# Loading the first FFN weights when the generation ends, and placing inverse units and x loads among the first f-tiles

## The chip, the cores and the metric

One NeuronCore of a Trainium2 chip runs the whole program. The metric is the time of one execution on the device in microseconds (us); the median of three runs is given. Engines are called PE (TensorE), ACT (ScalarE), DVE (VectorE), POOL (GpSimd) and SP (SyncE, which here only issues DMAs).

## The reference

Input `A_u` is 2048 tokens by 640 channels. Two residual blocks follow each other, each behind a layer norm with shift and scale computed from a condition vector `c`:

```python
h = _layernorm(x) * (1 + ca) + sa
x = x + ga * _A_ref(h, ...)      # S4D: causal convolution of h with a generated kernel K
h = _layernorm(x) * (1 + cb) + sb
x = x + gb * _B_ref(h, w1, w3, w2)   # SwiGLU
# A: K = 2 Re sum_n C[d,n] exp(A dt pos), y = irfft(rfft(h) * rfft(K)) + h * D_skip
# B: out = (silu(h @ w1) * (h @ w3)) @ w2      w1, w3: 640 x 1728, w2: 1728 x 640
```

All of it is float32.

## The kernel before

**Convolution.** The channels are taken in five pieces of 128. For each piece the convolution kernel is *generated* on POOL, ACT, DVE and PE (`gen_steps`, matmuls `kps`, L511). `k_steps` then takes its first transform (matmuls `pk`, L574; ACT copies them to `ko`, L578) and stores it to device memory (`k<-ko`, L581, eight DMAs per piece). `freq_steps` (18 steps per piece) loads the transformed input (`ht`) and the kernel (`kt`) back, transforms them further (`fa` L612, `fk` L626), multiplies (`fp`, L628), transforms back (`fa` L616), copies on ACT to `hz` (L618, three buffers) and stores `zd<-hz` (L621). The generation of one piece overlaps with the frequency steps of the piece before it. After the last generation only the last piece's `k` store, its `kt` load and its 18 frequency steps remain.

**Inverse.** The last transform goes by token blocks. A *unit* is two of sixteen groups of tokens: `inverse_load` fetches `iz<-zd` by four DMAs, `inverse` does 16 matmuls `iy` (L655) and adds them to `x2` on DVE (L660), which was loaded by `load_x2` (`x<-in_x`, four DMAs of 320 KB per block). Units 0 and 1, the token block 0, are done in part during the last piece's frequency steps (L927) and finished from `izb` after them. Units 2 and 3 (block 1) stand before the FFN; units 4 to 7 go among its f-tiles.

**FFN.** Four token blocks of 512. `ln2` normalises a block and turns it (`tp`, L692) into a high and a low half (`xh`, `xl`). For each block 14 f-tiles of 128 hidden features, in the order 0, 13, 1, 2, ..., 12 (13 is half a tile): `weights` loads `wr` (w1, w3) and `w2r`, and splits them on ACT (L670) and DVE (L671) into halves; `up` does 15 matmuls for each of w1 and w3 (L758 to L760, tiles `gu` in three PSUM banks); `gate` applies SwiGLU; `down` adds to five accumulators (`acc`, L793 to L799). Raw and split weights have two buffers each. `mid(b, i)` is called after every f-tile and puts inverse units and the next block's `ln2` in between. The weights of the first `WA = 2` f-tiles are loaded ahead.

**What sets the order.** Every instruction carries a priority, set by `self.at(v)`, and a scheduler with a model of the machine's times fixes each engine's order at build time; an engine then works strictly in that order. Lower numbers come first, and `last` is the last piece, number 4. Before the change the weights ahead stand at `1000 * last + 2500`, behind the frequency steps of the last piece (`+ 1000`). `order(a, b)` additionally keeps `a` behind `b` without a wait. All DMAs are issued by SP in one queue, and each issue waits until the one eight places before it has landed, since the DMAs share eight semaphores.

The inverse units' placement hangs on one constant, `IU`: units 2 to `IU - 1` stand before the FFN, the others are called from `mid`, where unit `m + 1` comes behind the f-tile at place `m`:

```python
for u in range(2, IU):
    self.inverse_unit(u, ip, po, None, 1, self.behind)
...
    if b == 0 and IU <= m + 1 < 8:
        self.inverse_unit(m + 1, ip, ps, "gu", 3)
```

Before the FFN the units use the banks of the accumulators (`po`); in `mid` they use the three `gu` banks.

Of the kernel before, what the change touches and what calls it, by code (L numbers as in the profile page):

```python
# [29 lines left out]
AE = '0101'  # L30
EG,EP,EH=[float(v) for v in '-730,-650,-750'.split(",")]
WA = int('2')
IU = int('4')
HU = [int(c) for c in '01234567']
MR = float('-850')
XB = int('4')
# [62 lines left out]
class K:  # L99
# [715 lines left out]
    def run(self):  # L815
# [9 lines left out]
        def open_(name, side=None, bufs=1, space=None):  # L825
            scopes[name] = ExitStack()
            return self.pool(name, bufs=bufs, space=space, ctx=scopes[name], side=side)
# [24 lines left out]
        last = self.param_turn(pp, psg, 0)  # L852
# [33 lines left out]
        last = NB - 1  # L886
# [21 lines left out]
        xp, ip, wp = open_("xp"), open_("ip"), open_("wp")  # L908
        self.x2 += [xp.tile([P, 4, D], F32, name=f"x2{b}") for b in range(1, 4)]
        self.ahead, self.turn = {}, 0  # L910
        mid_load = self.load
        self.at(1000 * last - 40)
        for st in self.k_steps(last, stp, kop, psg, KB, ip):
            st()
# [7 lines left out]
        for u in range(2):  # L922
# [7 lines left out]
            nc.vector.tensor_add(x2, py, x2)  # L930
            for j in (2 * u, 2 * u + 1):
                self.ln_part(stats[0], self.x2[0], j, 0, KT - 1)
        self.at(1000 * last + 2500)
        wload = self.load
        for m in range(WA):
            self.ahead[0, m] = self.weights(0, self.ORDER[m], wp, wload)
        self.at(1000 * last + 3000)
        close("fpool", "wbp", "kop", "ksp")
        pool = open_("ffn", "right")
# [1 line left out]
        po = open_("po", space=PSUM)  # L941
        ps = open_("ps", space=PSUM)
        z = self.inverse_load("izb", ip, "izb", 1, 0, 4, cut, D)
        for b in range(1, 4):
            self.load_x2(b, self.zload)
        self.inverse(0, 4, z, ps, "gu", 3, cut, D)
        nxt = {0: self.ln2(0, pool, ps, stats)}
        self.at(1000 * last + 4000)
        for u in range(2, IU):
            self.inverse_unit(u, ip, po, None, 1, self.behind)  # L950
        self.at(1000 * last + 5000)

        def mid(b, m):
            if b == 0 and IU <= m + 1 < 8:
                self.inverse_unit(m + 1, ip, ps, "gu", 3)
            if m == 8 and b < 3:
                nxt[b + 1] = self.ln2(b + 1, pool, ps)

        self.ffn(nxt, wp, pool, ps, po, mid)
        close("ps", "po", "ffn", "wp", "ip", "xp", "first")  # L960

# [29 lines left out]
```

## Time and profile before

| | |
|---|---|
| median of 3 runs | 1206.31 us (1205.34 to 1208.49) |
| the profiled execution | 1206.96 us, its span 1205.2 us |
| PE busy | 1029.8 us (85%) |
| DVE busy | 696.6 us (58%) |
| ACT busy | 495.2 us (41%) |
| POOL busy | 316.6 us (26%) |
| mean granted PE clock | 0.914 |

The generation ends at about 485 us, the last frequency steps end at 557 us, and the FFN's matmuls run from 582 us to the end. In a profile line, `out<-in` are tile names with buffer numbers left out, `[0.39 <-ACT hz L618]` is idle time before the instruction and what ended it, and SPq is SP's queue of DMA issues.

### The profile page before, as it was taken

How to read it: one execution, taken by the hardware profiler on the slowest of the kernel's cores; microseconds unless marked ns; L12 is line 12 of the kernel's file. 1: busy time of each engine (PE TensorE's matmuls, PEld its weight loads, DVE VectorE, ACT ScalarE, POOL GpSimd, SP SyncE). 2: the span in 40 equal slices, each digit the busy share in tenths (PEclk: the TensorE clock that was granted, in tenths of full speed). 3: DMA queues.
4: the chain of work that ended last, by engine and by line, in shares of the span. 5: the costliest groups of instructions: out<-in, count | busy, mean ns of one | idle time of the engine just before them, and what ended most of it. 6: DMA issues, size and time to landing. Idle time of an engine off the chain costs nothing.

```text
span 1205.2 us, 17828 instructions
## 1 busy us (share of the span) xinstructions
PE 1029.8 (85%) x6737; PEld 777.4 (65%) x6737; DVE 696.6 (58%) x1224; ACT 495.2 (41%) x768; POOL 316.6 (26%) x329
## 2 busy tenths in 40 slices
PE   2357673895996989895699999999999999999996
PEld 0134342673775857674376788888888888888885
DVE  7999979746866763143474484544745445354332
ACT  3456566436456573312242243432424333343221
POOL 5677768645757871000000000000000000000000
PEclk9578785797897988998699999999999999999999
DMA  9957648335365454778956333533335332353311
GB/s 265 232 160 222 184 125 220 86 104 116 95 172 112 114 117 122 175 187 218 214 142 155 97 88 88 136 96 86 97 88 133 108 95 74 84 143 98 98 44 44
DMA packets 206525, 157.61 MB, mean 131 GB/s; under 512 B 56680, under 2 KB 188648, under 8 KB 204776
## 3 DMA queue, kind: packets, MB, share of 16 engines
q1 hardware_dynamic: 206440, 156.48, 49.8%
q8 instruction: 53, 0.87, 0.3%
q14 instruction: 32, 0.26, 0.1%
HBM read 119.74 MB, written 36.70 MB: 130 GB/s over the span
## 4 chain that ended last, share of the span: by engine, by line
PE 70%; DVE 14%; DMA 7%; ACT 3%; issue 2%; SPq 2%; POOL 1%; DVEq 0%; ACTq 0%
PE gu L760 11%; PE gu L758 10%; PE gu L759 10%; PE fk L626 6%; PE fa L616 5%; PE acc L793 5%; PE acc L795 5%; PE acc L794 5%; PE fa L612 3%; PE kps L511 3%; PE iy L655 2%; DMA k<-ko 1%; DMA xt<-in_x 1%; DVE xs L258 1%; DVE step L446 1%
## 5 line engine op out<-in xcount | busy, mean ns | idle before, releaser
L758 PE MATMUL gu<-xh,wh 128*128 128x512 f32 x540 | 214.2, 397 | 0.5 <-ACT xh L695 0.5
L760 PE MATMUL gu<-xh,wl 128*128 128x512 f32 x540 | 213.9, 396 | 0.0
L759 PE MATMUL gu<-xl,wh 128*128 128x512 f32 x540 | 213.9, 396 | 0.0
L670 ACT ACTIVATE wh<-wr 128x640 fp32r<-128x640 f32 x108 | 74.2, 732 | 146.7 <-PE gu L759 134.5
L511 PE MATMUL kps<-yy,xx 128*32 128x64 f32 x2560 | 83.5, 247 | 53.3 <-DVE xx L503 28.3
L511 PEld LDWEIGHTS kps<-yy,xx 128*32 128x32 f32 x2560 | 61.6, 123 | 101.4 <-issue 53.9
L727 POOL MEMSET w2l<- 64x640 f32 x4 | 2.5, 626 | 469.0 <-PE acc L794 469.0
L758 PEld LDWEIGHTS gu<-xh,wh 128*128 128x128 f32 x540 | 101.7, 188 | 26.1 <-issue 1.0
L760 PEld LDWEIGHTS gu<-xh,wl 128*128 128x128 f32 x540 | 101.5, 188 | 26.4 <-issue 2.0
L759 PEld LDWEIGHTS gu<-xl,wh 128*128 128x128 f32 x540 | 101.6, 188 | 24.9 <-issue 0.5
L628 DVE TENSOR_TENSOR fp<-fk,hz 128x512 f32<-128x512 f32 x80 | 54.8, 686 | 98.1 <-PE fk L626 97.8
L626 PE MATMUL fk<-kt,wb 128*128 128x128 f32 x640 | 99.8, 305 | 13.1 <-DMA kt<-k 12.3
L626 PEld LDWEIGHTS fk<-kt,wb 128*128 128x128 f32 x640 | 90.6, 212 | 23.8 <-DMA kt<-k 7.6
L793 PE MATMUL acc<-ah,w2h 128*128 128x512 f32 x260 | 104.6, 402 | 0.0
L794 PE MATMUL acc<-ah,w2l 128*128 128x512 f32 x260 | 102.7, 395 | 0.0
L618 ACT ACTIVATE hz<-fa 128x512 f32<-128x512 f32 (+1 forms) x90 | 49.2, 547 | 126.5 <-PE fa L616 105.6
L487 POOL TENSOR_TENSOR yy<-e,e 128x512 f32<-128x512 f32 x80 | 87.0, 1109 | 42.7 <-PE kps L511 42.7
L795 PE MATMUL acc<-al,w2h 128*128 128x512 f32 x260 | 98.1, 395 | 0.0
L671 DVE TENSOR_TENSOR wl<-wr,wh 128x640 fp32r<-128x640 f32 x108 | 84.5, 817 | 16.6 <-ACT wh L670 16.6
L773 DVE SCALAR_TENSOR_TENSOR a<-th,gu 128x512 f32<-128x512 f32 x52 | 35.7, 687 | 100.3 <-ACT th L772 100.2
L774 DVE TENSOR_TENSOR a<-a,gu 128x512 f32<-128x512 f32 x52 | 35.7, 686 | 94.5 <-PE gu L760 94.5
L772 ACT ACTIVATE th<-gu 128x512 f32<-128x512 f32 x52 | 31.1, 598 | 139.5 <-PE gu L760 139.5
(190 smaller groups left out, 1801.2 us busy)
## 6 DMA issues: line engine op xcount, KB each, us to landing
wr<-in_w SPq DMA_DIRECT2D x104, 320.0 KB, 3.9
w2r<-in_w SPq DMA_DIRECT2D x52, 320.0 KB, 3.0
h<-ho SPq DMA_DIRECT2D x32, 320.0 KB, 4.5
k<-ko SPq DMA_DIRECT2D x40, 256.0 KB, 4.3
ht<-h SPq DMA_DIRECT2D x40, 256.0 KB, 2.8
kt<-k SPq DMA_DIRECT2D x40, 256.0 KB, 3.2
zd<-hz SPq DMA_DIRECT2D x80, 128.0 KB, 1.9
wm<-in_w_mod SPq DMA_DIRECT2D x10, 960.0 KB, 8.4
```

The lines of the kernel that those rows point to most:

```text
L487: G.tensor_tensor(out.rearrange("p d (k i) -> p d k i", k=4), bc(t1, 2, 4), bc(t2, 3, 8), op=ALU.mult)
L511: nc.tensor.matmul(kps[q * 32:(q + 1) * 32, e * 64:(e + 1) * 64], xx[:, r, i, :], yy[:, r, i, :, :].rearrange("p a b -> p (a b)"), start=( ...
L616: nc.tensor.matmul(pa[:, 1], self.wz[:, r, :], pp[:, r], start=(r == 0), stop=(r == 1))
L626: nc.tensor.matmul(pk[:, r, g], self.wb[:, 2 * i + g, r, :], kt[:, g0 + g, :], start=True, stop=True)
L670: self.nc.scalar.activation(H, v, AF.Copy)
L671: eng.tensor_tensor(Lo, v, H.bitcast(F32), op=ALU.subtract)
L758: nc.tensor.matmul(pg, wh[:, i, k, :], xh[:, k, :], start=(k == 0), stop=False)
L759: nc.tensor.matmul(pg, wh[:, i, k, :], xl[:, k, :], start=False, stop=False)
L760: nc.tensor.matmul(pg, wl[:, i, k, :], xh[:, k, :], start=False, stop=(k == KT - 1))
L793: nc.tensor.matmul(acc[k], w2h[:, sl], ah, start=(m == 0), stop=False)
L794: nc.tensor.matmul(acc[k], w2l[:, sl], ah, start=False, stop=False)
L795: nc.tensor.matmul(acc[k], w2h[:, sl], al, start=False, stop=(m == 12))
```

## The change

The weights of the first two f-tiles get the priority `1000 * last - 60`, just before `k_steps` of the last piece, and lose the order behind the last `kt` load. `IU` becomes 2, so that no inverse unit stands before the FFN, and units 2 and 3 are called from `mid` behind the f-tiles at places 1 and 2. The loads of x for blocks 1, 2 and 3 no longer stand between `izb` and the inverse of block 0, but before the FFN (block 1) and in `mid` at places 1 and 3 (blocks 2 and 3). In the program that results, SP issues the x loads of blocks 1 and 2, then the `iz` loads of units 2 and 3, then x of block 3.

```diff
-IU = int('4')
+IU = int('2')
...
         mid_load = self.load
+        self.at(1000 * last - 60)
+        for m in range(WA):
+            self.ahead[0, m] = self.weights(0, self.ORDER[m], wp)
         self.at(1000 * last - 40)
         for st in self.k_steps(last, stp, kop, psg, KB, ip):
             st()
...
-        self.at(1000 * last + 2500)
-        wload = self.load
-        for m in range(WA):
-            self.ahead[0, m] = self.weights(0, self.ORDER[m], wp, wload)
         self.at(1000 * last + 3000)
...
         z = self.inverse_load("izb", ip, "izb", 1, 0, 4, cut, D)
-        for b in range(1, 4):
-            self.load_x2(b, self.zload)
         self.inverse(0, 4, z, ps, "gu", 3, cut, D)
...
+        self.load_x2(1, self.zload)
+
         def mid(b, m):
+            if b == 0 and m in (1, 3):
+                self.load_x2((m + 3) // 2, self.zload)
             if b == 0 and IU <= m + 1 < 8:
                 self.inverse_unit(m + 1, ip, ps, "gu", 3)
```

## The prediction

> **What bounds the kernel now.** I read the chain that ended last first. TensorE (PE) carries most of it, so the question is where PE waits and whether the change reaches those places.
>
> ```profile
> PE 70%; DVE 14%; DMA 7%; ACT 3%; issue 2%; SPq 2%; POOL 1%; DVEq 0%; ACTq 0%
> ```
>
> The list of PE's waits, taken from 480 to 615 us, gives the places (who waited, for what, us in total, times, longest):
>
> ```profile
> PE iy L655 <- DMA izb<-zd: 10.1, 1, 10.1
> PE fk L626 <- DMA kt<-k: 5.6, 1, 5.6
> PE iy L655 <- DMA iz<-zd: 5.4, 1, 5.4
> PE tp L692 <- ACT xn L686: 5.3, 1, 5.3
> ```
>
> After 590 us PE is busy to the end, so each us by which that stretch starts earlier, or finishes with more done, is a us of the time. The chain from 425 to 700 us (start, duration, what) shows what stands in front of it:
>
> ```profile
> 507.00 4.23 DMA kt<-k
> ...
> 554.21 1.85 SPq L705
> ...
> 556.16 5.25 DMA zd<-hz
> ...
> 561.93 1.81 DMA zd<-hz
> ...
> 568.90 9.51 DMA x<-in_x
> 578.42 11.76 DMA iz<-zd
> 590.31 4.50 PE iy L655 x8
> ...
> 597.59 2.30 PE iy L655 x10
> ...
> 601.01 0.68 PE iy L655 x2
> ...
> 604.92 1.76 PE iy L655 x12
> ...
> 646.58 2.31 PE iy L655 x16
> ```
>
> The reader is to see three things: SyncE's queue (SPq) issuing a weight load (L705) directly ahead of the last zd stores; x loads of 9.5 us and iz loads of 11.8 us one behind the other; and 32 inverse matmuls (iy, L655) that PE takes at once, the first eight of them slowly.
>
> **Gain 1: the tail of the last frequency stage.** Before, the first two f-tiles' weights are loaded and split among its last steps. PE's timeline there:
>
> ```profile
> 541.59 1.05 PE L626 MATMUL fk<-kt,wb 128*128 128x128 f32 x8
> ...
> 543.78 1.05 PE L626 MATMUL fk<-kt,wb 128*128 128x128 f32 x8
> ...
> 554.33 1.05 PE L626 MATMUL fk<-kt,wb 128*128 128x128 f32 x8
> 555.22 2.15 PE L616 MATMUL fa<-fp,wz 128*128 128x256 f32 x8
> ```
>
> A step takes 543.78 − 541.59 = 2.19 us when nothing disturbs it. The four steps from 543.78 to 554.33 take 10.55 instead of 8.76 us. With the splits on ScalarE (ACT) and VectorE (DVE) gone from between them, **1.8 us** go.
>
> PE then ends this stage at 557.4, but ACT's last copy comes later, and SP issues the izb loads after it:
>
> ```profile
> 561.52 0.38 ACT L618 ACTIVATE hz<-fa 128x256 f32<-128x256 f32 x1 [2.88 <-DMA zd<-hz]
> ```
> ```profile
> 563.75 2.60 SPq L644 DMA_DIRECT2D izb<-zd  x4
> ```
>
> The copy waits for a buffer that a zd store still reads, and that store stood behind the weight load of 554.21. Without it the copy follows PE: 561.52 − 557.4 = 4.1 us, less some latency, I take **4.0 us**. Everything from izb to the first FFN matmul (DVE and ACT's layer norm, the transposes) moves forward unchanged; the 10.1 us wait shrinks by these 4.0.
>
> **Gain 2: units 2 and 3 leave the start of the FFN.** In the changed program PE goes through all 45 matmuls of f-tiles 0 and 13 before the first inverse matmul, and SP issues eight x loads instead of twelve ahead of that unit's iz loads. The 5.4 us wait for iz goes: its own four loads are done after twelve of 320 KB instead of sixteen, while PE comes to it some 12 us after its FFN start, not one. So **5.4 us**. The 32 inverse matmuls took 4.50 + 2.30 + 0.68 + 1.76 = 9.24 us; a unit of 16 among warm FFN matmuls takes 2.31, so two take 4.62: **4.6 us**.
>
> Against this stands the clock. FFN matmuls start slowly and become fast only after the iy rows:
>
> ```profile
> 582.38 0.79 PE L758 MATMUL gu<-xh,wh 128*128 128x512 f32 x1 [0.49 <-ACT xh L695]
> 582.97 0.63 PE L759 MATMUL gu<-xl,wh 128*128 128x512 f32 x1
> 583.40 0.63 PE L760 MATMUL gu<-xh,wl 128*128 128x512 f32 x1
> ...
> 595.33 0.39 PE L758 MATMUL gu<-xh,wh 128*128 128x512 f32 x1
> 595.56 0.39 PE L759 MATMUL gu<-xl,wh 128*128 128x512 f32 x1
> ```
>
> Spacing is 0.43 us slow and 0.23 fast; from 590.31 PE needed 5.0 us of unbroken work to reach the fast one. By 606.7 (604.92 + 1.76), counting the two programs' order of instructions, 32 FFN and 32 inverse matmuls were done: 606.7 − 582.4 = 24.3 us, of which 24.3 − 5.4 − 9.2 = 9.7 for the FFN ones. After: 5.0 us slow hold 11.6 of them, the other 20.4 take 4.8, so 9.8 us: a loss of **0.1 us**. If the slow stretch ran to 8.5 us the loss would be 1.7. [...]
>
> **Loss 1: where the loads now land.** They are moved to the end of generation, in SP's queue ahead of zd of step 10; the loads of f-tiles 1 and 2 follow as buffers come free, among the k stores. Their sizes, from the issues between 540 and 557 us:
>
> ```profile
> wr<-in_w SPq DMA_DIRECT2D x6, 320.0 KB, 6.5
> w2r<-in_w SPq DMA_DIRECT2D x3, 320.0 KB
> ...
> wr<-in_w SPq DMA_DIRECT2D x2, 160.0 KB
> w2r<-in_w SPq DMA_DIRECT2D x2, 160.0 KB, 6.4
> ```
>
> That is 11 × 320 KB = 3.60 MB. All of it is now queued before the last k store, and all k stores must land before kt can be loaded, for which PE already waits 5.6 us. So every us that the k stores lose is a us on PE. What the DMA engines had free there, by stretches (PE, PEld, DVE, ACT, POOL busy, clock, DMA share, GB/s):
>
> ```profile
> 484.50:493.00 8.50, 8.50 (x42) 6.28 (x43) 1.48 (x3) 4.32 (x6) 0.00 (x0) 1.00 0.44 106
> 493.00:505.00 12.00, 12.00 (x61) 9.11 (x60) 2.77 (x4) 4.25 (x7) 0.00 (x0) 1.00 0.94 197
> 541.00:556.00 15.00, 14.22 (x86) 12.12 (x84) 7.88 (x12) 6.71 (x11) 0.00 (x0) 1.00 0.93 252
> ```
>
> PE's last matmuls of the generation, which let the weights' memory go, are these:
>
> ```profile
> 484.06 0.44 PE L511 MATMUL kps<-yy,xx 128*32 128x64 f32 x12
> ```
>
> So the loads can be issued from 484.5. From 493 on the engines are full; before, 8.5 × 0.56 = 4.8 us are free. At 252 GB/s, the rate where these same loads run today, 3.60 MB take 14.3 us; less 4.8, the k stores and kt come **9.5 us** later. I take this value because its row is that of the same transfers. At 197 GB/s, the rate beside k stores, it is 18.3 − 4.8 = 13.5. Below, the loads could hide wholly (0) if the engines had more room than their share shows. Five splits each are put into ACT's and DVE's queues ahead of ko and fp; at 0.7 us (1.37 for two in ACT's row below) they delay ko by some 3.4 us. In SP's queue the zd stores, ht loads and k stores stand behind loads that wait for a free buffer. Both delays lie inside the wait for the k stores, so I add nothing for them; if the DMA engines were idle meanwhile, they would count (the third rival).
>
> [...]
>
> **Loss 2: PSUM in the FFN.** Unit 2 now takes the three gu banks right behind f-tiles 0 and 13. Its second half needs the bank of f-tile 13, which DVE's L782 frees. Rows of ACT and of DVE:
>
> ```profile
> 609.72 1.37 ACT L670 ACTIVATE wh<-wr 128x640 fp32r<-128x640 f32 x2 [2.60 <-PE gu L759]
> ```
> ```profile
> 607.90 0.48 DVE L660 TENSOR_TENSOR x<-iy,x 128x320 f32<-128x320 f32 x1
> ...
> 613.29 0.69 DVE L782 TENSOR_TENSOR a<-u,gu 64x512 f32<-64x512 f32 x1
> ```
>
> ACT's first row starts when f-tile 13's matmuls end, so its bank is free 613.98 − 609.7 = 4.3 us later, after the change with two adds (L660) more on DVE in front, 5.3. PE has 4 inverse matmuls (0.6) and 15 of the down projection (3.5) in between: a wait of 5.3 − 4.1 = **1.2 us**. From 0, if DVE takes the adds later, to 3, if unit 3 meets it as well. The x loads of blocks 2 and 3 and the iz loads of units 4 on are needed 20 us or more after they are issued: nothing. POOL's clearing of a piece of w2l moves with the weights and POOL is idle there: nothing.
>
> **Sum.** 1.8 + 4.0 + 5.4 + 4.6 = 15.8 gained; 0.1 + 9.5 + 1.2 = 10.8 lost; net −5.0 us. The profiled execution took 1206.96 us (span 1205.2), 0.65 above the median of 1206.31, so 1201.96 in its terms and **1201.3** as a median.
>
> **Rivals.** *Early loads are free*: they go into the idle engines and kt loses 3 us at most, by the share of 0.44. For it: in the chain kt's issue at 507 hangs on SP's queue as well as on the last store. Against: full engines from 493. Time: 1206.3 − 15.8 + 0.1 + 3 + 0 = 1193.6. [...]
>
> *It evens out*: loads run at 197 GB/s (13.5) and the FFN's start waits 3: 0.8 us slower, 1207.1. For it: those k stores, at that rate, are the neighbours.
>
> *Slower: SP's queue*. A load waits in the queue for a buffer that a split must free, and k stores stand behind it while DMA engines idle. SP's row of such a wait today:
>
> ```profile
> 544.65 2.66 SPq L705 DMA_DIRECT2D w2r<-in_w  x2
> ```
>
> With the 1.85 of the chain, 4.5 us of waiting, none of the idle 4.8 used, and 197 GB/s: 18.3 + 4.5 = 22.8 us for kt, net −15.8 + 0.1 + 22.8 + 1.2 = +8.3, so 1214.6. It is slower beyond what can be told apart once kt loses over 18.1 us (15.8 − 1.3 + 3.6). Against: up to eight DMAs can be under way at once, so engines seldom run dry.
>
> *The change does not take*: excluded, the program's order shows loads and units moved.
>
> **How the numbers follow.** About 0.3% (3.6 us) is what a measurement can tell from no change: below 1202.7 is faster, above 1209.9 slower. Forecast 0.54 (kt late by 6 to 13 us, 1197.8 to 1204.8; three quarters of it faster), free 0.13, even 0.16, slower 0.17. Faster 0.41 + 0.13 = 0.54; same 0.13 + 0.16 = 0.29; slower 0.17. For 8 in 10, the range runs from the free case's 1194 to 1210, leaving about a tenth on either side.
>
> **What would show it.** Right: the last frequency stage steps at 2.19 us to its end, izb is issued within 3 us of PE's last fa, no wait for iz at the first FFN matmuls, and PE's wait for kt grows from 5.6 to about 15. Wrong: a kt wait under 9 or over 20, new PE waits of more than 3 us in the first f-tiles, or zd stores late again at the end of the last stage.

## The result and the profile after

The changed kernel takes 1198.88 us (median of four runs, 1197.58 to 1200.46), the kernel before beside it 1207.05 (four runs, 1205.34 to 1208.49): a ratio of 0.9933, with a 95% interval of 0.9915 to 0.9952. By the ratio that is 8.1 us faster, 5.8 to 10.3 by the interval, where 5.0 was forecast. The profiled execution after took 1198.77 us, its span is 1197.0, 8.2 less than before.

PE's share of the chain that ended last, and PE's waits from 480 to 615 us, after:

```profile
PE 70%; DVE 15%; DMA 7%; ACT 3%; issue 2%; POOL 1%; SPq 1%; DVEq 0%; ACTq 0%; POOLq 0%
```
```profile
PE fk L626 <- DMA kt<-k: 11.5, 1, 11.5
PE iy L655 <- DMA izb<-zd: 6.0, 1, 6.0
```

The wait for kt has doubled (5.6 before), that for izb has lost 4.1 us, and that for iz (5.4) is gone. PE's share of the chain is the same as before (70%); only the waits, place by place, tell what happened.

Five rows of PE's timeline divide the program around the change: the last `kps` of the generation, the first `fk` of the last piece, its last `fa`, the `iy` fed by izb, and the first FFN matmul. Two of them before, which the prediction doesn't show:

```profile
511.36 2.05 PE L626 MATMUL fk<-kt,wb 128*128 128x128 f32 x8 [5.55 <-DMA kt<-k]
...
567.43 3.53 PE L655 MATMUL iy<-izb,wd 128*64 128x128 f32 x16 [10.07 <-DMA izb<-zd]
```

All five after, with a few rows from between:

```profile
483.94 0.44 PE L511 MATMUL kps<-yy,xx 128*32 128x64 f32 x12
...
518.33 2.05 PE L626 MATMUL fk<-kt,wb 128*128 128x128 f32 x8 [11.48 <-DMA kt<-k]
...
557.45 1.05 PE L626 MATMUL fk<-kt,wb 128*128 128x128 f32 x8
...
559.64 1.05 PE L626 MATMUL fk<-kt,wb 128*128 128x128 f32 x8
560.53 2.15 PE L616 MATMUL fa<-fp,wz 128*128 128x256 f32 x8
568.71 3.16 PE L655 MATMUL iy<-izb,wd 128*64 128x128 f32 x16 [6.03 <-DMA izb<-zd]
...
583.29 0.79 PE L758 MATMUL gu<-xh,wh 128*128 128x512 f32 x1 [0.49 <-ACT xh L695]
...
596.32 1.30 PE L655 MATMUL iy<-iz,wd 128*64 128x320 f32 x8
...
601.24 1.30 PE L655 MATMUL iy<-iz,wd 128*64 128x320 f32 x8
```

Subtracting neighbours gives the table that the rest of this text uses. The last column is the sum: last `kps` to the end of the span. It leaves out what lies ahead of the last `kps`, where the profiled executions differ by several us (it starts between 480.0 and 487.1).

| us | A: kps to fk | B: to last fa | C: to izb's iy | D: to first gu | E: to the end | sum |
|---|---|---|---|---|---|---|
| before | 27.3 | 43.9 | 12.2 | 15.0 | 622.8 | 721.1 |
| after | 34.4 | 42.2 | 8.2 | 14.6 | 613.7 | 713.1 |
| change | +7.1 | −1.7 | −4.0 | −0.4 | −9.1 | −8.1 |

Of the 7.1 us in A, 5.9 are a longer wait for kt. Another 1.1 are a wait before the `fa` at 505.28, behind DVE's `fp` and ACT's `hz`, whose buffer a zd store held until 503.8 (in the chain below). The frequency stage now steps by 2.19 us to its end (557.45 to 559.64). Both rows of unit 2 (596.32 and 601.24) come without idle time before them. The chain of waits after shows what A is made of:

```profile
486.48 5.60 DMA wr<-in_w
492.16 0.74 ACT wh L670
...
493.29 5.70 DMA k<-ko
499.00 4.80 DMA zd<-hz
...
503.90 0.61 ACT hz L618
...
509.24 4.83 DMA k<-ko
514.14 4.05 DMA kt<-k
...
562.71 0.39 ACT hz L618
563.12 1.81 DMA zd<-hz
564.95 0.58 SPq L644
```

Between the last generation matmul and kt there is now hardly any PE in the chain: weight loads, splits on ACT and k stores wait for one another. The end of the stage is clean: ACT's last copy starts at 562.71, when PE's last `fa` ends (560.53 + 2.15), and izb is issued 2.3 us after that.

### The profile page after: what moved, and what is told of

It reads as the page before. It is cut to its first block, busy times and chain, and to the rows that moved or that the text cites. A ratio compares the mean times of both kernels' runs of the same rounds, so it can differ in the third digit from the quotient of the medians.

```text
span 1197.0 us, 17830 instructions
## 1 busy us (share of the span) xinstructions
PE 1023.3 (85%) x6737; PEld 775.0 (65%) x6737; DVE 697.5 (58%) x1224; ACT 494.9 (41%) x768; POOL 316.5 (26%) x329
## 4 chain that ended last, share of the span: by engine, by line
PE 70%; DVE 15%; DMA 7%; ACT 3%; issue 2%; POOL 1%; SPq 1%; DVEq 0%; ACTq 0%; POOLq 0%
PE gu L758 11%; PE gu L759 11%; PE gu L760 11%; PE fk L626 6%; PE acc L793 5%; PE fa L616 5%; PE acc L794 5%; PE acc L795 5%; PE fa L612 3%; PE kps L511 3%; DMA k<-ko 2%; PE iy L655 1%; DMA xt<-in_x 1%; DVE xs L258 1%; DVE yy L502 1%
## 5 line engine op out<-in xcount | busy, mean ns | idle before, releaser
L511 PE MATMUL kps<-yy,xx 128*32 128x64 f32 x2560 | 83.0, 245 | 54.6 <-DVE xx L503 29.4
L758 PEld LDWEIGHTS gu<-xh,wh 128*128 128x128 f32 x540 | 102.0, 189 | 27.6 <-issue 1.5
L626 PEld LDWEIGHTS fk<-kt,wb 128*128 128x128 f32 x640 | 90.3, 211 | 27.6 <-issue 13.9
L487 POOL TENSOR_TENSOR yy<-e,e 128x512 f32<-128x512 f32 x80 | 87.1, 1110 | 42.1 <-PE kps L511 41.7
```

The source lines that it names most:

```text
L487: G.tensor_tensor(out.rearrange("p d (k i) -> p d k i", k=4), bc(t1, 2, 4), bc(t2, 3, 8), op=ALU.mult)
L511: nc.tensor.matmul(kps[q * 32:(q + 1) * 32, e * 64:(e + 1) * 64], xx[:, r, i, :], yy[:, r, i, :, :].rearrange("p a b -> p (a b)"), start=( ...
L626: nc.tensor.matmul(pk[:, r, g], self.wb[:, 2 * i + g, r, :], kt[:, g0 + g, :], start=True, stop=True)
L758: nc.tensor.matmul(pg, wh[:, i, k, :], xh[:, k, :], start=(k == 0), stop=False)
```

## The experiments

A ratio is to the kernel before, run beside it. Absolute times in an expectation assume 1207.2 us for that kernel; the later groups of runs have it at 1203.84, 1204.88 and 1204.47, so there differences are compared.

### The two halves of the change, alone

Weights at the end of the generation, units and x as before:

```diff
# against the changed kernel
-IU = int('2')
+IU = int('4')
...
+        for b in range(1, 4):
+            self.load_x2(b, self.zload)
...
-        self.load_x2(1, self.zload)
...
-            if b == 0 and m in (1, 3):
-                self.load_x2((m + 3) // 2, self.zload)
```

> The kernel before with one part of the change: the first two f-tiles' weights at the end of generation, units 2 and 3 and the x loads as they were. Theory (terms that add up by stage: tail of the last frequency stage -5.7 us, wait for kt +7.0, both as read from the two traces): +1.3 us over before, PE's wait for kt about 12 us, its wait for izb about 6, its wait for iz still about 5. Rival (the kt wait is longer only because of something the other part does to the queue, so early loads cost nothing): kt wait 5.6 us, -5.7 us against before.

Measured: 1208.48 us against 1207.17, ratio 1.0016 (0.9999 to 1.0034), as the first theory had it. PE's waits:

```profile
PE fk L626 <- DMA kt<-k: 12.1, 1, 12.1
...
PE iy L655 <- DMA iz<-zd: 5.8, 1, 5.8
```

Units and x moved, the weights left in the last frequency stage:

```diff
# against the changed kernel
-        self.at(1000 * last - 60)
-        for m in range(WA):
-            self.ahead[0, m] = self.weights(0, self.ORDER[m], wp)
...
+        self.at(1000 * last + 2500)
+        wload = self.load
+        for m in range(WA):
+            self.ahead[0, m] = self.weights(0, self.ORDER[m], wp, wload)
```

> The changed kernel with the weights put back among the last frequency steps: only units 2 and 3 and the x loads are moved. Theory: the FFN's start gains its 9.1 to 9.4 us by itself and the k stores are left alone: about -9.2 us against before, kt wait 5.6, izb wait 10, no iz wait; some 1.5 us faster than the change as a whole. Rival (the FFN's start gains only because the weights are out of the way before izb): iz or weight waits in the first f-tiles return, and less than 5 us is gained.

Measured: 1196.28 us, ratio 0.9907 (0.9885 to 0.9929): 11.2 us less where 9.2 was expected. PE's waits:

```profile
PE iy L655 <- DMA izb<-zd: 8.8, 1, 8.8
PE fk L626 <- DMA kt<-k: 5.6, 1, 5.6
...
PE fk L626 <- ACT hz L618: 1.7, 1, 1.7
```

| us | A | B | C | D | E | sum |
|---|---|---|---|---|---|---|
| weights alone | 35.0 | 42.7 | 8.1 | 14.6 | 622.9 | 723.3 |
| units and x alone | 27.4 | 44.1 | 10.9 | 14.9 | 612.7 | 710.0 |

The gain is that of the units and x. The early weights give back at kt what they save at the stage's end, and a little more; leaving them where they were is 3 us better by the sum (713.1 less 710.0), of which 1.0 lies in E and is put down to the clock's timing in the last section. The two ratios' intervals overlap, so the whole times alone don't decide between this version and the change.

### Fewer bytes ahead of the k stores

Of the 3.60 MB, 1.97 belong to f-tiles 1 and 2, which follow as buffers come free. Their loads held behind izb:

```diff
-                wh, wl, w2h, w2l = ... or self.weights(b, m, wp)
+                wh, wl, w2h, w2l = ... or self.weights(b, m, wp, self.zb if b == 0 and i < 4 else None)
```

(`self.zb` is the last izb load.)

> The changed kernel, with the weight loads of f-tiles 1 and 2 held in the queue until after the izb loads, so that 1.64 MB instead of 3.60 MB stand ahead of the last k store; the five splits each on ScalarE and VectorE stay where the change put them. Theory (the DMA engines' bytes set the delay of kt): 1.64 MB at 252 GB/s is 6.5 us, less 4.8 free, so kt waits 5.6 + 1.7 = 7.3 us instead of 11.5 to 12 and the time is some 5 us under the change, 1194. Rival (the splits in front of ko and the queue's waits for them delay the k stores): kt waits as in the change, time 1199. A new cost may come in if the weights of f-tile 1 land too late for its first matmul, at about 590 us.

Measured: 1197.02 us, ratio 0.9918 (0.9899 to 0.9938). The profiled execution is the longest of the seven (1202.36 us). A is 29.3, B 42.3, C 8.3, D 14.6, E 619.1, the sum 713.5. The kt wait is 7.5, where the bytes theory, with the prediction's own 252 GB/s and 4.8 us of room, has 7.3. A new wait has come:

```profile
PE fk L626 <- DMA kt<-k: 7.5, 1, 7.5
...
PE gu L758 <- DVE a L782: 5.3, 1, 5.3
```
```profile
576.39 1.73 SPq L705 DMA_DIRECT2D wr<-in_w  x2
```

SP issues f-tile 1's weights at 576.39 only, behind x and the first iz loads. The next version issues them first:

```diff
+        self.rawa = {(0, i): self.raws(0, self.ORDER[i], wp, self.zload) for i in (2, 3)}
         self.inverse(0, 4, z, ps, "gu", 3, cut, D)
```

(`raws` is the part of `weights` that loads; the splits stay where they were.)

> The changed kernel, but the loads of f-tiles 1 and 2 (1.97 MB) are issued right behind izb and ahead of the x loads, while those of the first two f-tiles (1.64 MB) stay at the end of the generation. Against the earlier run that held the same loads back but left them behind x and iz (a 5.3 us wait for f-tile 1's gate chain). Bytes theory: first fk comes 2.0 us later after the last generation matmul than before, as there (29.3 instead of 27.3); the stage's end and the izb wait save 1.8 and 4.0, the moved inverses save 9.1, and the wait in the FFN is gone: 1207.2 + 2.0 - 5.8 - 9.1 = 1194.3. Rival (the loads behind izb only push x and iz back): 1.97 MB at about 250 GB/s is 7.9 us later for iz2, so an iz or x wait of 2 to 6 us in the first f-tiles, 1197 to 1200.

Measured: 1192.07 us against 1203.84, ratio 0.9905 (0.988 to 0.9929), 11.4 us less where 12.9 was expected. PE's waits:

```profile
PE fk L626 <- DMA kt<-k: 7.7, 1, 7.7
PE iy L655 <- DMA izb<-zd: 6.1, 1, 6.1
```

A 29.4, B 41.7, C 8.3, D 14.6, E 613.9: the sum is 707.9, the shortest of all, and the wait in the FFN is gone. Then only the first f-tile's 0.98 MB left early:

```diff
-WA = int('2')
+WA = int('1')
...
-... for i in (2, 3)}
+... for i in (1, 2, 3)}
```

> The version that gained most so far (first two f-tiles' weights at the end of the generation, those of f-tiles 1 and 2 right behind izb), with only the first f-tile's weights (0.98 MB) left at the end of the generation; the second f-tile's 0.66 MB go behind izb with the rest. Room theory (before, the 27.4 us between the last generation matmul and the first fk hold 6.9 us in which the engines are free; 3.68 MB beyond before's took 13.4 us of them, 1.75 MB took 6.9): 0.98 MB need 3.6 to 3.9 us, so the first fk comes 0 to 0.8 us later than before (27.3 to 28.1) instead of 2.0; the rest as there (fk to the last fa 41.7, to izb 8.3, to the first FFN matmul 14.6, FFN 613.9): 1.2 to 2.0 us less from the last generation matmul to the end than the 707.7 of that version, 705.7 to 706.5. Rival (the second f-tile's weights come too late behind izb): a wait of 1 us or more in f-tile 13, and the FFN 1 to 3 us longer.

Measured: 1196.73 us against 1204.88, ratio 0.9932 (0.9905 to 0.9959). A is 29.2, B 42.4, C 8.4, D 16.4, E 615.9, the sum 712.3. The expectation failed twice. 0.98 MB cost as much in A as 1.64, and with the engines less busy there (a share of 0.85 against 0.94 in the two versions above), so this loss isn't bytes less room; and the rival's cost came, 1.8 in D and 2.0 in E. On A, ACT's rows of before and of this version agree in one thing:

```profile
489.53 1.02 ACT L578 ACTIVATE ko<-pk 128x1024 f32<-128x1024 f32 x1 [2.01 <-PE pk L574]
```
```profile
489.89 0.74 ACT L670 ACTIVATE w2h<-w2r 128x640 fp32r<-128x640 f32 x1 [0.23 <-DMA w2r<-in_w]
490.53 1.92 ACT L578 ACTIVATE ko<-pk 128x1024 f32<-128x1024 f32 x2
```

The first `ko` copy stands behind a split that waits for its load: it starts 6.8 us after the last `kps` (483.74), before 5.5 us (484.06). With 1.64 MB early and the next loads right behind izb it is 6.9 us, as in the changed kernel. That SP's queue then carries this 1.3 us on to kt, and so makes the floor of 2 us, is argued from the order, not shown by a run.

### Weights in the last frequency stage

With the first two f-tiles late in that stage, and f-tiles 1 and 2 behind izb (the diffs above together):

> The version with the moved inverses alone (first two f-tiles' weights late in the last frequency stage, 1196.3 measured), and the loads of f-tiles 1 and 2 right behind izb ahead of x instead of in the last frequency stage. Bytes theory: the kt wait stays at 5.6; of the 3.61 MB that the last stage carried 1.64 MB are left, issued at about 543 to 548 and landed by about 553, so most of the 1.8 + 4.0 us of the stage's end is saved too: 1192 (izb wait about 6 instead of 8.8). Rival (it is the loads of the first two f-tiles that slow the end, since they lie there): the end saves under 1.5, 1195 or more. Second rival: what is saved comes back as an iz or x wait of 2 to 6 us in the first f-tiles, 1195 to 1199.

Measured: 1195.14 us, ratio 0.9921 (0.9893 to 0.995): 9.5 us less where 15 was expected. A 27.6, B 44.0, C 8.3, D 14.7, E 614.0, the sum 708.7. C came down by all 3.9, B by nothing: one `fk` (550.35) waits 1.1 us for an `hz` copy. With the units alone, where these loads lie in the same place, `hz` copies stand behind splits that wait 1.2 and 2.5 us for their loads. The same with the first loads released at the fourth-last kt load:

```diff
-        wload = self.load
+        wload = self.loads[-4]      # the kt loads in order
```

> As the run before, but the loads of the first two f-tiles are released by the fourth-last kt load of the last frequency stage (about 526 us) instead of the last one (about 542), where the DMA engines are busy 0.43 to 0.78 of the time. Bytes theory: kt wait 5.6, no new fk wait over 1 us, the whole 5.8 us of the stage's end is saved and the 9.1 of the inverses: 1192 less up to 1, so 1191. Rival (the last four pairs of h and k tiles are delayed by the 1.64 MB issued ahead of them): fk waits of 2 to 5 us for kt in the stage, 1194 to 1196.

Measured: 1196.26 us, ratio 0.994 (0.9918 to 0.9961): 7.2 us less where 16 was expected. A 27.6, B 46.9, C 8.3, D 14.9, E 612.9, the sum 710.6. And so without holding anything behind izb:

> The version with the moved inverses alone, with the weights' loads released by the fourth-last kt load of the last frequency stage and nothing held behind izb: 3.61 MB go out between about 526 and 545 among the last h and k tiles. Bytes theory: no bytes lie between the last generation matmul and the first fk, so kt wait 5.6; the engines have room for about 0.4 x 16 us x 250 GB/s = 1.6 MB there, so the rest delays either the last h and k tiles or the end: the end saves 2 to 4, fk waits under 2: 1193 to 1195. Rival (a load issued ahead delays every later one by its whole bytes, as after the generation): fk waits of 5 to 8 us, about 1200.

Measured: 1196.06 us, ratio 0.9942 (0.9922 to 0.9963): 7.0 us less where 12 to 14 was expected. A 27.5, B 48.0, C 8.3, D 15.2, E 611.4, the sum 710.3. B is 3 to 4 us longer than before in both. The rivals had waits of 2 to 8 us for kt there, which did not come. PE and ACT in the first of the two (its lines are one further down):

```profile
534.75 1.16 PE L627 MATMUL fk<-kt,wb 128*128 128x128 f32 x8 [1.51 <-ACT hz L619]
```
```profile
533.48 0.74 ACT L671 ACTIVATE w2h<-w2r 128x640 fp32r<-128x640 f32 x1 [1.42 <-DMA w2r<-in_w]
534.12 0.58 ACT L619 ACTIVATE hz<-fa 128x512 f32<-128x512 f32 x1
```

The split waits 1.42 us for its load, the `hz` copy that stands behind it in ACT's order starts right after it, and PE waits 1.51 us for that copy. In the two versions PE's waits for `hz` come to 2.6 and 2.8 us (0.8 before). So a good part of what B loses is splits placed ahead of `hz` before their data is there, though the loads were moved to where the DMA engines had time to spare (shares of 0.43 to 0.78 from 527 to 543 us with the units alone). Where the rest goes is not shown, and no run has the loads there without splits.

### What the loss at kt is made of

Other loads in the same place: the version with the weights late, and all twelve x loads (3.93 MB) at the end of the generation, without any split.

```diff
+        self.at(1000 * last - 60)
+        for b in range(1, 4):
+            self.load_x2(b, mid_load)
```

> The units-only kernel (weights among the last frequency steps) with all twelve x loads (3.93 MB) put at the end of generation, ahead of the k stores, in the place the change gives to the weights: as many bytes, no split on any engine. Theory (bytes): with the 7.0 us that 3.60 MB cost in the change, 3.93 MB cost about 8 (11 at 252 GB/s), kt waits 13 to 16 us and the time is about 1205. Rival (splits and the queue's waits for them): kt waits 6 to 7 us, time about 1198.

Measured: 1208.03 us, ratio 1.0013 (0.9993 to 1.0032). A is 39.0, 11.7 more than before; B 44.0, C 12.3, D 14.6, E 611.3, the sum 721.1. The waits, though, are not those expected:

```profile
PE fk L626 <- DMA kt<-k: 8.3, 1, 8.3
PE fk L626 <- ACT hz L618: 6.6, 2, 5.4
```

Only 2.7 of the 11.7 us are at kt. The longest wait for `hz`, 5.4 us, lies in A too (506.79): the copy needs a buffer whose zd store is issued at 495.33, behind the x loads. A wait of 1.6 for `fp` and 2.0 more of PE's busy time, at a lower clock (0.87 against 0.97), make up the rest. So no split is needed for the loss, zd stores that are pushed back cost as well as k stores, and here the whole gain of the units is lost. The x loads also hold SP's queue for 9.6 us, so this run does not tell bytes from the order of the queue.

Then, on the version that gained most, a first load of f-tiles 1 and 2 into the later x's space, so that 3.61 MB of weights lie in one row ahead of the k stores:

```diff
+        for i in (1, 2):                       # space of x2[i], overwritten later
+            for j, src in enumerate((self.w1, self.w3)):
+                ... dma_start(<5 x 128 of x2[i]>, src[:, f0:f0 + P].rearrange("(k p) f -> p k f", p=P))
+            ... dma_start(self.x2[i][:, 1, :], self.w2[f0:f0 + P, :])
```

> The version that holds f-tiles 1 and 2 behind izb, with 1.97 MB more at the end of the generation: the weights of f-tiles 1 and 2 are loaded a first time there, ahead of every k store, into the space of the later x (nothing reads them; the x loads overwrite them later), so that with the first two f-tiles' 1.64 MB all 3.61 MB lie ahead of the k stores in one row, where the changed kernel has 1.64 MB ahead and the rest among the stores. What it tells is the wait for kt alone. Rate theory (the loss is bytes over the rate at which these weights move, 275 GB/s or more, less the 6.5 us of free room, wherever they lie): 3.61 / 275 = 13.1, less 6.5 to 6.9, so the first fk comes 33.5 to 34.5 us after the last generation matmul, as in the changed kernel (34.4). Place theory (the loss was 7.1 instead of 9.5 because half the bytes lay among the stores): 36 to 38 us.

Measured, in a single execution: A is 35.1, against 34.4 in the changed kernel; its time is 1202.85. That lies in neither range, and nearer to the rate theory. Between these two executions the place, among or ahead of the stores, made 0.7 us. The stretch A by windows (stretch, length, PE busy, clock, DMA share, GB/s), of before, of the changed kernel, of x early and of this version:

```profile
484.06:511.36 27.30, 21.75 (x117) 0.97 0.75 171
```
```profile
483.94:518.33 34.39, 21.77 (x118) 0.88 0.99 244
```
```profile
485.09:524.05 38.96, 23.70 (x117) 0.87 0.99 222
```
```profile
485.48:520.57 35.09, 23.54 (x118) 0.85 0.99 239
```

Before, 0.25 × 27.30 = 6.8 us of engine time were free, and 27.30 × 171 = 4.67 MB were moved in 0.75 × 27.30 = 20.5 us. After, 34.39 × 244 = 8.39 MB in 34.0 us: 3.72 MB more took 13.6 us more, 274 GB/s. 13.6 − 6.8 = 6.8 us, nearly the 7.1 measured. The x loads: 8.65 − 4.67 = 3.98 MB in 38.6 − 20.5 = 18.1 us, 220 GB/s; 18.1 − 6.8 = 11.3, measured 11.7. So 3.98 MB of x took 18.1 us of the engines, 3.72 MB of weights 13.6. That these sums come out is no test of them: each rate is taken from the stretch whose length it gives back, and with a share of 0.99 it must. What the lines show is that the engines were full.

Last, whether the form of the x loads sets their rate: two DMAs over 128 partitions for each block, instead of four over 32, once at the end of the generation and once behind izb. The second text's "run before" is the version with only the first f-tile's weights early (1196.73 us).

```diff
-        for q in range(4):
-            ... dma_start(self.x2[b][q * 32:(q + 1) * 32], self.xv[q, :, 4 * b:4 * b + 4, :])
+            for j in range(2):
+                ... dma_start(self.x2[b][:, 2 * j:2 * j + 2, :], self.xv[:, :, 4 * b + 2 * j:4 * b + 2 * j + 2, :])
```

> The version with the x loads at the end of the generation (first fk 38.96 us after the last generation matmul, 1208.0 measured), with the same 3.93 MB in six DMAs over 128 partitions instead of twelve over 32. If the rate of a load's form decides (220 GB/s there): at 290 GB/s they take 13.6 us of the engines, of which 6.5 are free, so the first fk comes 34 to 35 us after, and the time falls by 4 to 5. If bytes alone decide, or the source: 38.5 to 39.5 and no change.

> As the run before, with the x of each later token block loaded by two DMAs over all 128 partitions (1280 numbers of a partition each) instead of four over 32 (2560 each). Where nothing in the first f-tiles waits for x, as the versions before show, neither theory has it faster or slower by over 1 us in the FFN; what it tells is the rate of these loads when they run behind izb (220 GB/s at a busy share of about 1.0 in the form of 32 partitions). If the form sets the rate, it rises towards the 330 to 360 GB/s of the f-tile weights; if not, it stays at 210 to 240.

Measured: at the end of the generation, in a single execution, 1228.09 us, with A at 61.7; behind izb 1226.39 us, ratio 1.0197 (1.0164 to 1.0229). Both theories are wrong: the rate does hang on the form (220 GB/s in the form of 32 partitions, 100 here), and the other way round. While these loads ran at the end of the generation:

```profile
484.00:504.00 20.00, 12.22 (x50) 0.94 0.26 100
```

100 GB/s, with a share of 0.26 of the engines' time in use, as much as 0.26 × 16 = 4.2 engines. Here A is longest while the engines have most room: PE waits once 27.5 us for `hz` and once 9.0 for kt, and the zd and k stores behind these waits stand in SP's queue after the loads. Behind izb, the iz loads stand in SP's queue after them, and PE waits 19.4 us for iz.

## Why the prediction was right, and by how much it missed

**Gain 1** held by its own mechanism: 1.8 forecast for the undisturbed steps, 1.7 measured in B; 4.0 forecast for the zd stores that stood behind a weight load, 4.0 measured in C. The version with the first two f-tiles' weights late and the next two's behind izb shows that C needs only f-tiles 1 and 2 out of the way. B needs the splits of the first two out of the way as well, as ACT's rows before show, where an `hz` copy stands behind a split that waits for its load:

```profile
545.24 0.74 ACT L670 ACTIVATE wh<-wr 128x640 fp32r<-128x640 f32 x1 [2.86 <-DMA wr<-in_w]
545.89 0.58 ACT L618 ACTIVATE hz<-fa 128x512 f32<-128x512 f32 x1
```

**Gain 2 and its losses**: 5.4 + 4.6 − 0.1 − 1.2 = 8.7 forecast, 9.1 measured in E, and the half with the units alone has 10.1 (622.8 less 612.7). The wait for iz is gone. That the sum came so near is in part luck: without Loss 2, which did not come, it is 9.9 (5.4 + 4.6 − 0.1), and the clock's term depends on when the FFN happens to start. PE's matmuls came at the fast spacing about 5.2 us after the FFN's start:

```profile
588.35 0.33 PE gu L759
588.68 0.24 PE gu L760
```

The granted clock was 0.50 up to 588.4 and 1.00 from there on, so the slow stretch was 5.1 us, near the 5.0 of before. With the units alone it was 3.0 us and with x early 0, so this agreement is chance, and 5.0 us is not, as the prediction has it, an amount of work that PE needs (the last section has the reason). The wait for a PSUM bank (**Loss 2**, 1.2) did not come: unit 2's second half starts at 601.24 without idle time, before the L782 that was to free its bank (601.36 to 602.05). So that start did not hang on L782, as the prediction has it; why it did not is open. The low bound, 0, was the true one.

**Loss 1** is the term that was mis-sized: 9.5 forecast, 7.1 measured, the kt wait 11.5 instead of about 15 (inside the 9 to 20 that were given as its bounds). Its kind was right: full DMA engines (0.99), k stores pushed back, PE waiting for it. Its two numbers are the rate, 252 GB/s, and the free room, 4.8 us; which of them was off is not settled. Taken from the two stretches afterwards, the added bytes moved at 274 GB/s in place of 252, and the free room up to the first `fk` was 6.8 us in place of 4.8, since the count had ended at 493 us: 13.6 − 6.8 in place of 14.3 − 4.8. But the same pair gives no loss at all for 1.64 MB (6.0 less 6.8), where 2.0 was measured and the prediction's pair gives 1.7; and used ahead of a run, with all weights in one row, it gave 33.5 to 34.5 for A, which was 35.1. The 2 us that even 0.98 MB cost fit neither pair. There the prediction's delay of `ko` by the splits, for which it added nothing, is the likely cause: the first `ko` copy comes 1.3 us later.

**The rivals.** "Early loads are free" would have kt lose 3 us at most: refuted by 7.1, and by the weights alone, which gain nothing (1.0016): here transfers that PE waits for are queued behind the early loads. "SP's queue" (22.8 us at kt) is far off, but its mechanism exists: splits that wait for their load delay `ko` (1.3 us), and `hz` in the versions with the loads in mid-stage (2.6 and 2.8 us on PE). "It evens out" came true of the x loads: they lost 11.7 us and the gain with them (1.0013).

By the table the change is worth 3.1 us more than forecast (8.1 against 5.0): 2.4 in A, 0.4 in E, 0.4 in D, less 0.1 in B.

**The best version** measured has the first two f-tiles' weights early and those of the next two right behind izb: ratio 0.9905, sum 707.9. By whole times it is not told apart from the units and x alone (0.9907); by the sums it is 2 us ahead of that, and 5 ahead of the change.

## What to carry to other kernels

Before a load is moved forward, look at which transfers come behind it in the queue and who waits for them: price it as its bytes over the rate that this kind of load reached, less the engine time that is free until the waiting transfer. That is a rough price: here such sums were off by 0.3 to 2.4 us for the weights. Count the instructions that consume the load as well: here a split that waited 1.42 us for its load held back the `hz` copy behind it, and PE waited 1.51 us for that copy. When a change has two halves, run each alone, since here one half earned the gain and the other, alone, earned nothing (1.0016). And before a difference of 1 or 2 us between two versions is explained, look whether the slow stretch of the clock has the same length in both.

## What the runs showed of the hardware that was not expected

**The granted clock changed on a grid of its own.** In the traces of before and of the changed kernel it is 0.50 or 1.00, and every stretch of one value that lies wholly inside the trace (36 and 34 of them) lasts a whole multiple of 3.413 us; before, the last ones ahead of the fast stretch from 595.30 on are 10.24 us slow, 3.413 fast and 20.48 slow. In both the FFN starts inside a slow stretch, and how long its matmuls stay slow (0.43 us apart instead of 0.235) differs from version to version: 12.9 us before, and 0 to 5.1 in the versions below. A us of the slow stretch costs 1 − 0.235 / 0.43 = 0.45 us. Taken off E, that leaves the same time in five versions in which PE waits for the same in the FFN:

| us | E | slow from the FFN's start | E less 0.45 of it |
|---|---|---|---|
| after | 613.7 | 5.1 | 611.4 |
| units and x alone | 612.7 | 3.0 | 611.3 |
| loads in mid-stage, f-tiles 1 and 2 held | 612.9 | 3.3 | 611.4 |
| loads in mid-stage, nothing held | 611.4 | 0 | 611.4 |
| x early | 611.3 | 0 | 611.3 |

So the differences between their E are the clock's timing and not the edits' doing. In some other versions more is left (612.4 in the best one, where PE has a new wait of 0.5).

**The rate differed by over a factor of three between forms of load.** Three stretches with the engines fed by one kind alone or nearly so: in the best version the weights of f-tiles 1 and 2 (128 partitions), then x (32 partitions a DMA), and above x in 128 partitions.

```profile
564.00:568.00 4.00, 0.04 (x1) 0.50 1.15 348
573.00:577.00 4.00, 3.51 (x12) 0.50 1.02 218
```

348, 218 and 100 GB/s (the profile gives shares a little over 1 here). The second has the engines busy all the time at 0.63 of the first rate, the third leaves them idle for most of it (a share of 0.26). The iz loads, over 64 partitions each, ran at 237 GB/s and a share of 1.04 (before, 588 to 592 us). Why each form has its rate is not shown: the weights and x differ in their source as well, and no run here took a cause away by itself.
